# Issuing V from ACT's queue beside K on SP's queue in a streaming attention kernel

## The chip, the cores and the metric

The kernel runs on one core of a Trainium2 chip. The metric is the device time of one launch in microseconds (us). Ratios are computed as the mean time of one kernel's runs over the mean of the other's runs of the same rounds, so they are not quite the ratios of the medians that are quoted.

## The reference, cut to what matters

```python
# x: (2, 1, 512); k_cache, v_cache: (2, 32, 8192, 128), bf16
xn = layernorm(x)
q  = (xn @ wq).reshape(2, 1, 32, 128).transpose(0, 2, 1, 3)
p  = softmax(einsum("bhqd,bhkd->bhqk", q, k_cache) * 128 ** -0.5)
o  = einsum("bhqk,bhkd->bhqd", p, v_cache)
return x + merge_heads(o) @ wo + relu(xn @ w1) @ w2
```

It is a decode step: one query per batch and head, against 8192 keys and values. The two caches are 268 MB, the weights about 12 MB, and every byte is used once. So the question is how well the transfers are kept going.

## The kernel before

The 64 heads are done in 32 pairs. For each pair, K is 4 MB and V is 4 MB, each loaded by one transfer of 128 rows of 32 KB. There are two buffers for K (`ks`) and two for V (`vs`). TensorE works in steps: step t transposes K of pair t, computes the scores, and in its second half does the weighted sum with V of pair t-1. SP issues the transfers:

```python
load_k(0); load_k(1); load_v(0)
for t in range(NP - 2):                 # NP = 32
    sp.wait_ge(pT[NG - 1], t + 1)       # transposes of pair t are done: its K buffer is free
    load_k(t + R)                       # R = 2
    sp.wait_ge(sW, t + 1)               # weighted sum in step t is done: a V buffer is free
    load_v(t + 1)
sp.wait_ge(sW, NP - 1)
...                                     # V of pair 31 in two halves, then wo in five pieces
```

TensorE's step and its tail, cut:

```python
pe.wait_ge(dK[r], n16)                  # K of this pair has landed
for e in range(NG):
    transposes(r, e)
    if e >= 2: scores(r, e - 2, n)
values(v, n, n16)                       # waits for the softmax and for V of the pair before
weighted(v, 0) ...                      # and the last two groups of scores
# after the loop: two small sums, weighted(V of pair 31), transposes, product with wo
```

ACT's loop, in which the softmax of a pair and the copy of the result before it are done:

```python
with a.Fori(0, NP // R) as tr:
    for r in range(R):
        a.reg_add(reg, reg, 1)
        pair(r, reg, tr * R + r)        # ends with out_copy, which waits for sW
```

## Time and profile before

| | before |
|---|---|
| time, median of all runs of the first comparison | 661.0 us (660.82 to 661.77, 6 runs) |
| span of the profiled run | 658.7 us |
| bytes read | 280.5 MB, on one DMA queue |
| period of a step, from step 6 on | 19.43 us |
| TensorE's wait for K | 67.8 us in 27 waits |

The prediction shows the lines. The DMA engines are busy from start to end, and TensorE waits a little for K in nearly each step. When reading such a page, look at what remains after the last large transfer has landed: only there does TensorE's work show in the time.

### The profile page before, as it was taken

The page shows a single profiled execution, that of the slowest core. Times are in us where ns is not written, and L with a number is a line of the kernel's source. Part 1 is how long each engine was busy: PE and PEld are TensorE (multiplying, and loading weights), DVE is VectorE, ACT ScalarE, POOL GpSimd, SP SyncE. Part 2 cuts the span into 40 slices and gives each one's busy share as a digit, 9 for nine tenths or more (in the row PEclk, how much of TensorE's full clock was granted, in tenths as well). Part 3 has the DMA queues.
Part 4 walks back from the last instruction along what each step waited for, and adds up shares of the span by engine and source line. Part 5 has one row for each costly group of instructions (what it writes and reads, how often), then busy time and mean ns, then how long its engine had stood idle before and what let it go on. Part 6 is the DMA issues. An engine that isn't in the chain of part 4 may idle for free.

```text
span 658.7 us, 26859 instructions
## 1 busy us (share of the span) xinstructions
PE 559.9 (85%) x12737; PEld 536.7 (81%) x12737; DVE 253.2 (38%) x436; ACT 255.8 (39%) x403; POOL 8.8 (1%) x46
## 2 busy tenths in 40 slices
PE   2897799998889978789878878987888898878897
PEld 0497798987889978789878878987888898878896
DVE  1144344443434434334433434443334443434341
ACT  1034344443433534244353434434343434433340
POOL 1000000000000000000000000000000000000000
PEclk9889999998998989899988989898899988989996
DMA  8999999999999999999999999999999999999996
GB/s 365 433 440 420 439 428 431 436 426 438 422 442 422 440 432 428 438 424 442 420 442 424 436 436 426 438 422 442 424 438 430 430 438 424 440 422 442 424 425 282
DMA packets 10542, 280.66 MB, mean 426 GB/s; under 512 B 1186, under 2 KB 1188, under 8 KB 1700
## 3 DMA queue, kind: packets, MB, share of 16 engines
q1 hardware_dynamic: 10528, 280.50, 99.1%
q8 instruction: 9, 0.15, 0.1%
q14 instruction: 1, 0.01, 0.0%
q10 hardware_dynamic: 4, 0.00, 0.0%
HBM read 280.50 MB, written 0.00 MB: 426 GB/s over the span
## 4 chain that ended last, share of the span: by engine, by line
DMA 58%; PE 37%; ACT 2%; issue 1%; SPq 1%; ACTq 0%; DVE 0%
DMA ks<-in_A_k_cache_dram 54%; PE tp L288 21%; PE Sc L295 11%; PE ot L308 4%; DMA w_sb<-in_A_wo_dram 4%; ACT kT L415 2%; ACT L415 1%; SPq L190 0%; PE Sc L343 0%; SPq L185 0%; PE Sc L346 0%; SPq L173 0%; SPq L172 0%; SPq L166 0%; PE ot L400 0%
## 5 line engine op out<-in xcount | busy, mean ns | idle before, releaser
L288 PE MATMUL tp<-identb,ks 128*128 128x128 bf16 x4096 | 323.4, 228 | 67.8 <-DMA ks<-in_A_k_cache_dram 67.8
L415 DVE COPY kT<-tp 128x1024 bf16<-128x1024 bf16 x320 | 219.7, 691 | 323.8 <-PE tp L288 323.5
L288 PEld LDWEIGHTS tp<-identb,ks 128*128 128x128 bf16 x4096 | 255.0, 102 | 71.6 <-DMA ks<-in_A_k_cache_dram 71.5
L415 ACT COPY kT<-tp 128x1024 bf16<-128x1024 bf16 x192 | 194.3, 1012 | 231.2 <-PE tp L288 231.2
L295 PE MATMUL Sc<-q,kT 128*128 128x64 bf16 x4096 | 217.1, 196 | 9.3 <-ACT kT L415 6.1
L295 PEld LDWEIGHTS Sc<-q,kT 128*128 128x128 bf16 x4096 | 178.8, 100 | 13.1 <-ACT kT L415 9.6
L308 PE MATMUL ot<-prm,vs 128*128 128x64 bf16 x4224 | 157.6, 193 | 3.3 <-issue 3.3
L308 PEld LDWEIGHTS ot<-prm,vs 128*128 128x128 bf16 x4224 | 140.5, 98 | 6.2 <-issue 3.6
L528 ACT COPY nm<-Sc 128x2 f32<-128x2 f32 x32 | 5.1, 160 | 119.8 <-PE Sc L346 119.8
L532 ACT ACTIVATE prm<-Sc,nm 64x128 bf16<-64x128 f32 x64 | 25.7, 401 | 4.4
L469 DVE TENSOR_REDUCE mcol<-Sc 64x1 bf16<-64x128 f32 x64 | 18.6, 291 | 20.0 <-PE Sc L295 19.5
L415 ACT ACT_TABLE_LOAD x16 | 20.5, 1283 | 2.2
L243 PE MATMUL ot<-vs,xz 128*16 128x512 bf16 x32 | 8.6, 436 | 8.1 <-DMA vs<-in_A_wq_dram 8.1
L474 DVE TENSOR_REDUCE mx<-Sc 1x2 bf16<-1x128 bf16 x32 | 8.9, 279 | 16.9 <-PE Sc L343 16.9
L520 ACT COPY OTf<-ot 128x2 f32 x32 | 5.1, 160 | 26.1 <-PE ot L308 26.1
L243 PEld LDWEIGHTS ot<-vs,xz 128*16 128x16 bf16 x32 | 3.1, 99 | 13.1 <-issue 10.4
L228 POOL COPY q<-qb 128x2 bf16<-128x2 bf16 x32 | 5.8, 184 | 590.1 <-PE Sc L295 568.2
L532 ACT ACTIVATION_READ_ACCUMULATOR prm<-Sc,nm x64 | 11.8, 185 | 0.0
L445 DVE TENSOR_SCALAR qs<-ot 16x512 bf16<-16x512 f32 x1 | 0.7, 678 | 16.5 <-PE ot L243 16.5
L343 PE MATMUL Sc<-identb,mcol 128*1 128x128 bf16 x32 | 7.0, 217 | 0.0
L346 PE MATMUL Sc<-mx,onesb 1*128 1x2 bf16 x32 | 5.5, 172 | 0.0
L400 PE MATMUL ot<-OX,w_sb 128*128 128x2 bf16 x128 | 4.0, 166 | 1.1 <-DMA w_sb<-in_A_wo_dram 0.7
(56 smaller groups left out, 38.0 us busy)
## 6 DMA issues: line engine op xcount, KB each, us to landing
ks<-in_A_k_cache_dram SPq DMA_DIRECT2D x32, 4096.0 KB, 26.7
vs<-in_A_v_cache_dram SPq DMA_DIRECT2D x31, 4096.0 KB, 31.3
vs<-in_A_wq_dram SPq DMA_DIRECT2D x1, 4096.0 KB, 12.1
vs<-in_A_v_cache_dram SPq DMA_DIRECT2D x2, 2048.0 KB, 19.0
w_sb<-in_B_w_dram SPq DMA_DIRECT2D x2, 1792.0 KB, 17.9
w_sb<-in_A_wo_dram SPq DMA_DIRECT2D x1, 1792.0 KB, 25.1
w_sb<-in_A_wo_dram SPq DMA_DIRECT2D x1, 896.0 KB, 26.8
w_sb<-in_A_wo_dram SPq DMA_DIRECT2D x1, 768.0 KB, 28.2
```

The source lines that it names most:

```text
L228: g.tensor_copy(q2[t % R][:], qb[:, 2 * t:2 * t + 2]).then_inc(sQ1, 1)
L243: i = pe.matmul(qp, lhsT=xz[:, kt, Z - g * Bsz:Z - g * Bsz + QG * Bsz], rhs=vs[1][:, (kt * QG + g) * 512:(kt * QG + g + 1) * 512], start=( ...
L288: t = pe.transpose(tp[e % 4][:, i, :], ks[r][:, kk * Dh:(kk + 1) * Dh], identb[:])
L295: t = pe.matmul(Sc[r][:, 2 * kk:2 * kk + 2 * REP], lhsT=kT[e % 4][:, i, :], rhs=rep(q2[r][:]), start=True, stop=True,)
L308: t = pe.matmul(ot[r][:, 0:2 * REP], lhsT=vs[r][:, kk * Dh:(kk + 1) * Dh], rhs=rep(prm[r][:, kk, :]), start=(kk == 0), stop=(kk == KB - 1),)
L343: pe.transpose(tr_of(r), mcol[r][:], identb[:]).then_inc(sT, 1)
L346: pe.matmul(bc_of(r), lhsT=onesb[:], rhs=mx[r][:], start=True, stop=True).then_inc(sB, 1)
L415: fn(kT[e % 4][:], tp[e % 4][:]).then_inc(kR[e], 1)
L469: m = v.tensor_reduce(out=mcol[i][half, :], in_=S_of(i)[half, :, u], axis=AX.X, op=ALU.max)
L474: v.tensor_reduce(out=mx[i][:], in_=tr_of(i).rearrange("o (u m) -> o u m", u=2), axis=AX.X, op=ALU.max, negate=True,).then_inc(sX, 1)
L520: a.copy(OTf[:, bass.ds(c, 2)], ot[r][:, 0:2]).then_inc(sO, 1)
L532: x = a.activation(out=prm[i][half, :, u], in_=S_of(i)[half, :, u], func=ACTF.Exp, bias=nm[i][half, u:u + 1], scale=1.0, accum_out=RS[half ...
```

## The change

The intent is to put the two streams on two queues, so that V is issued by ACT, which has just waited for the same event, and SP has K alone. The whole diff, with some lines of its context cut:

```diff
@@ -177,8 +177,6 @@
         for t in range(NP - 2):
             sp.wait_ge(pT[NG - 1], t + 1)
             load_k(t + R)
-            sp.wait_ge(sW, t + 1)
-            load_v(t + 1)
         sp.wait_ge(sW, NP - 1)
@@ -543,10 +541,16 @@
-        with a.Fori(0, NP // R) as tr:
+        with a.Fori(0, NP // R - 1) as tr:
             for r in range(R):
                 a.reg_add(reg, reg, 1)
                 pair(r, reg, tr * R + r)
+                a.dma_start(
+                    vs[1 - r][:], V_all[bass.ds((tr * R + r + 1) * P, P), :]
+                ).then_inc(dV[1 - r], 16)
+        for r in range(R):
+            a.reg_add(reg, reg, 1)
+            pair(r, reg, NP - R + r)
```

## The prediction

> **What bounds the kernel now.** I read the page's slices and queues first, then the chain that ended last, then the timelines of the issuing queue and of TensorE. The slices and queues (tenths of busy time, GB/s, then packets, MB and share of 16 engines' span for each queue):
>
> ```profile
> DMA  8999999999999999999999999999999999999996
> GB/s 365 433 440 420 439 428 431 436 426 438 422 442 422 440 432 428 438 424 442 420 442 424 436 436 426 438 422 442 424 438 430 430 438 424 440 422 442 424 425 282
> q1 hardware_dynamic: 10528, 280.50, 99.1%
> q10 hardware_dynamic: 4, 0.00, 0.0%
> ```
>
> The DMA engines are full from the second slice to the last but one, at some 430 GB/s, and 99.1% of the engines' span went to one queue, SP's. ACT's queue (q10) carried only the small x load. The chain and the waits say who feels it:
>
> ```profile
> DMA 58%; PE 37%; ACT 2%; issue 1%; SPq 1%; ACTq 0%; DVE 0%
> PE tp L288 <- DMA ks<-in_A_k_cache_dram: 67.8, 27, 3.4
> ks<-in_A_k_cache_dram SPq DMA_DIRECT2D x32, 4096.0 KB, 26.7
> vs<-in_A_v_cache_dram SPq DMA_DIRECT2D x31, 4096.0 KB, 31.3
> ```
>
> TensorE waits for K 27 times, 67.8 us in all. It never waits for V. One step in the middle (start, duration, what; in brackets the idle time before it and its releaser):
>
> ```profile
> 314.64 1.34 PEld L288 LDWEIGHTS tp<-identb,ks 128*128 128x128 bf16 x24 [2.29 <-DMA ks<-in_A_k_cache_dram]
> ...
> 325.59 0.33 SPq L161 DMA_DIRECT2D ks<-in_A_k_cache_dram  x1
> ...
> 330.70 0.33 SPq L164 DMA_DIRECT2D vs<-in_A_v_cache_dram  x1
> 330.80 0.16 ACT L520 COPY OTf<-ot 128x2 f32 x1 [0.70 <-PE ot L308]
> 331.10 1.28 ACT L415 ACT_TABLE_LOAD   x1
> 334.07 2.48 PEld L288 LDWEIGHTS tp<-identb,ks 128*128 128x128 bf16 x24 [3.52 <-DMA ks<-in_A_k_cache_dram]
> ```
>
> A step starts at 314.64 when K has landed; the next starts at 334.07, 19.43 us later. Between them K and V move 2 x 4.194 MB, so the rate is 8.389 MB / 19.43 us = 431.8 GB/s and one 4 MB transfer takes 9.71 us. TensorE itself needs 16.06 us of the step (314.64 to 330.70). K is issued 10.95 us into the step, V at its end. All the steps from 139.81 us on have this period, within a few hundredths. The kernel is a stream of bytes; TensorE has about 2 to 3.5 us of slack per step. The tail matters too (TensorE's weight loads):
>
> ```profile
> 625.47 1.34 PEld L288 LDWEIGHTS tp<-identb,ks 128*128 128x128 bf16 x24 [2.32 <-DMA ks<-in_A_k_cache_dram]
> ...
> 641.85 0.52 PEld L363 LDWEIGHTS Sc<-RS,onesh 128*128 128x128 f32 x4 [0.48 <-issue]
> 642.41 0.96 PEld L366 LDWEIGHTS ot<-ident,ys 2*128 2x128 f32 x8
> 643.39 5.42 PEld L308 LDWEIGHTS ot<-prm,vs 128*128 128x128 bf16 x128
> ...
> 650.46 2.27 PEld L400 LDWEIGHTS ot<-OX,w_sb 128*128 128x128 bf16 x84 [0.44 <-DVE OX L501]
> 653.34 0.71 PEld L400 LDWEIGHTS ot<-OX,w_sb 128*128 128x128 bf16 x24 [0.62 <-DMA w_sb<-in_A_wo_dram]
> 654.26 0.40 PEld L400 LDWEIGHTS ot<-OX,w_sb 128*128 128x128 bf16 x12 [0.21 <-DMA w_sb<-in_A_wo_dram]
> 654.90 0.29 PEld L400 LDWEIGHTS ot<-OX,w_sb 128*128 128x128 bf16 x8 [0.24 <-DMA w_sb<-in_A_wo_dram]
> ```
>
> When the last K lands (625.47), three 4 MB transfers are still to come: V of pair 30, V of pair 31 and wo. 625.47 + 3 x 9.71 = 654.6, and the last wo piece lets TensorE go at 654.90. So TensorE's last work hides under the stream except for the last 3.8 us (span 658.7).
>
> **What the Trainium skill says.** (1) "DMA: Bandwidth & Descriptors", section "Issuing engines are not separate DMA queues": transfers started by SP, ACT or GpSimd run on the same 16 engines and interleave; issuing from several saves only the sequencer's issue time. The trace agrees in what it can show: an issue takes 0.33 us of SP's otherwise waiting queue, so there is nothing to save. (2) The same page, "Where 436 GB/s comes from": a ceiling of 435.2 GB/s for this fabric. The trace's 431.8 is within 0.8% of it. (3) The same page, "Queues, rings and completion order": each engine goes round-robin between the queues that have work, a packet at a time; and a completion increment lands only after all earlier writes of that engine, over its queues. The trace of before cannot show the first, having one busy queue only. I take it as equal halves, since the rows of K and V are equally long (32 KB).
>
> **The change, part by part.**
>
> Removed: 30 waits and 30 issues of V from SP. SP issues V after the wait for the same event (end of the weighted sum), which TensorE produces in order with the event for K. So SP's order never holds a K up behind a V wait: K was issued at 325.59, as the transposes ended, and V at 330.70, as the weighted sum ended. Worth 0.
>
> Added on ACT: per pair one issue. ACT's one DMA in this trace took 0.56 us, plus registers for the address; I estimate 0.5 to 0.8 us. It stands after the OTf copy (330.80 + 0.16), and ACT's next needed act is the first kT copy, some 0.7 us after TensorE restarts at 334.07. From 331.0: issue to 331.7, table load 1.28 us to 333.0. It is ready before 334.8. Worth 0 in the K-bound steps; V is issued about 0.5 us later than before, harmless with 31.3 us to landing. In the first steps, where TensorE is not yet waiting for K, the table load at 73.68 stood on the path, so one or two steps may lose about 0.5 us. Those steps regain it at the first K wait.
>
> Moved: the order of the bytes, and this is what counts. One queue is strict: K(t+2) goes before V(t+1). Check: from the start of step 0 at 32.82, the transfers up to K6 are eleven: 32.8 + 11 x 9.71 = 139.6; the first long run of K waits starts at 139.81. With two queues, K and V share, so V is served earlier and K later, while the total is the same.
>
> Worked from the issue times of before (K at 64.43, 85.26, 101.10; V at 52.33, 73.27, 90.36, 106.22): V0 is done at 52.2. K2 and V1 then share and end at about 71.6. V2 comes at 73.9, so K3 has 2.3 us alone and its other 7.4 us at half rate, 14.8 us: 88.7, still before the step needs it at 90.4. V2 has 2.3 us left and ends at 93.3; K4, which had 2.3, needs 14.8 more: 108.1. Step 3 ends at 106.2, so step 4 is the first to wait for K, where before it was step 6. From there both queues always have work, and each K takes 19.43 us. Last K: 108.3 + 27 x 19.43 = 632.9, against 625.47: 7.4 us later. V then lands at about K's landing + 4.6 us and is needed about 11 us after it, so V still makes nobody wait.
>
> Tail: the bytes end when they ended, at about 654.6. But TensorE's work after the last K, which was hidden, no longer is. From before: 625.47 to 641.37 the last step, 15.9; to 643.39, 2.0; V of pair 31, 5.42 and 0.38; to 650.46, 1.27; wo, 2.27 + 0.71 + 0.40 + 0.29 = 3.67; the end, 3.47. Sum 32.1. 632.9 + 32.1 = 665.0 against 658.7: +6.3 us. V31 would land at about 645 and wo at 654.6, before TensorE reaches them (about 651 and 658), so this sum has no DMA wait in it. By the sum: 660.88 + 6.3 = 667.2. I shade it to 666.0, because the share of K may exceed a half, and because a rate nearer to the 435 ceiling has a small chance.
>
> **Rivals.** (a) Nothing moves: the arbiter lets K's queue drain first, or the bytes alone decide. For: 99.1% of one queue, same bytes. Against: the tail argument needs only that V gets some earlier service. Time 660 to 661. (b) V is served first whenever it has work: then the whole of V30 stands before the last K, 9.71 us: 625.5 + 9.7 + 32.1 = 667.3 span, +8.6, 669.5 us. This bounds the ordering effect. (c) Two streams lower the rate (packet switches, two regions of HBM at once). One per cent of the roughly 525 us of K-bound steps is 5 us, on top: about 671; 2% would be 677. Nothing in this trace speaks for it, and nothing can against it, as no two large transfers on different queues meet here. (d) Two rings overlap better and reach 435.2: the steps shrink 0.8%, 4 us, giving about 663. (e) ACT's issue holds the kT copies up in each step: at most 0.8 us in 32 steps would be 26 us, but the 2.3 to 3.5 us idle before each K swallows it.
>
> **Range and chances.** Faster by 2% (under 647.7) would need more than the ceiling allows: 280.5 MB / 435.2 GB/s is 644.5 us before start and end are added. Chance 0.01. Slower by 2% (over 674.1) needs (c) at about 1.2% or more on top of the tail; 0.08. The range goes from (a), 660.5, to (b) with some loss of rate, 672.
>
> **What would show it.** ACT's queue should hold about 126 MB (30 x 4.19). K's time from issue to landing should stay near 27 us in the steady steps, V's fall from 31.3 to about 26, K waits start at step 4 (near 108 us), the period stay 19.43 us, and the last K land near 633. In the tail no wait for wo should be left: the chain ends in TensorE's L308 and L400. It is wrong if the period changes by over 0.1 us (rate), if the last K lands at 625 (no sharing), or if TensorE waits for V or for ACT's kT copies in the steady steps.

## The result, and the profile after

The changed kernel took 665.18 us (665.14 to 666.03, 6 runs), against 661.0 us before: ratio 1.0065, 95% interval 1.0052 to 1.0078. It is 4.2 us slower. The prediction said 666.0, in a range of 660.5 to 672.0.

The slices and queues of the changed kernel (as before: tenths busy, GB/s, then packets, MB and share of the engines' span), and its two large groups of issues (KB each, median us from issue to landing):

```profile
DMA  8999999999999999999999999999999999999994
GB/s 361 438 431 435 424 435 434 425 435 433 427 435 435 423 439 427 431 439 427 431 439 427 431 437 429 431 435 429 433 435 427 433 437 423 437 433 427 435 420 170
q1 hardware_dynamic: 6208, 154.67, 54.4%
q10 hardware_dynamic: 4324, 125.83, 44.1%
ks<-in_A_k_cache_dram SPq DMA_DIRECT2D x32, 4096.0 KB, 26.7
vs<-in_A_v_cache_dram ACTq DMA_DIRECT2D x30, 4096.0 KB, 28.6
```

ACT's queue now carries 125.83 MB (30 x 4.19). The rate in the slices is what it was, until the last slice: 170 GB/s where before it was 282, because the span now ends later than the bytes. K still takes 26.7 us to land; V takes 28.6 us instead of 31.3.

The first wait for K in the changed kernel, one step in the middle with ACT's issue, and the start of the last step (start, duration, what; in brackets the idle time and its releaser):

```profile
107.25 1.34 PEld L286 LDWEIGHTS tp<-identb,ks 128*128 128x128 bf16 x24 [0.49 <-DMA ks<-in_A_k_cache_dram]
...
319.04 0.34 ACTq L548 DMA_DIRECT2D vs<-in_A_v_cache_dram  x1
320.94 1.50 PEld L286 LDWEIGHTS tp<-identb,ks 128*128 128x128 bf16 x24 [2.31 <-DMA ks<-in_A_k_cache_dram]
...
340.36 1.34 PEld L286 LDWEIGHTS tp<-identb,ks 128*128 128x128 bf16 x24 [2.27 <-DMA ks<-in_A_k_cache_dram]
...
631.79 1.72 PEld L286 LDWEIGHTS tp<-identb,ks 128*128 128x128 bf16 x24 [2.41 <-DMA ks<-in_A_k_cache_dram]
649.28 0.52 PEld L361 LDWEIGHTS Sc<-RS,onesh 128*128 128x128 f32 x4 [0.39 <-issue]
...
650.82 3.96 PEld L306 LDWEIGHTS ot<-prm,vs 128*128 128x128 bf16 x128
...
656.42 3.27 PEld L398 LDWEIGHTS ot<-OX,w_sb 128*128 128x128 bf16 x128 [0.44 <-DVE OX L499]
```

The period is 340.36 - 320.94 = 19.42 us, as before; over all 27 steps from 107.25 to 631.79 it is 19.43. So no rate was lost. But the last K lands at 631.79 instead of 625.47, 6.3 us later, and from there TensorE's tail (31.3 us to the end at 663.1) is no longer hidden: the product with wo runs as one group of 128 without a wait for a piece of wo. The stretches of the end (us, then busy time of PE, PEld, DVE, ACT and POOL, the share of TensorE's full clock that it was granted, share of the DMA engines, GB/s), for the kernel before:

```profile
650.00:655.00 5.00, 3.86 (x127) 3.49 (x125) 0.23 (x1) 0.00 (x0) 0.00 (x0) 0.62 0.70 277
655.00:658.60 3.60, 0.55 (x9) 0.28 (x9) 0.38 (x2) 0.00 (x0) 0.00 (x0) 0.50 0.01 3
```

and for the changed kernel:

```profile
650.00:655.00 5.00, 4.90 (x136) 4.76 (x136) 0.79 (x3) 0.00 (x0) 0.00 (x0) 1.00 0.71 283
655.00:660.00 5.00, 3.93 (x134) 3.55 (x134) 0.77 (x4) 0.00 (x0) 0.00 (x0) 1.00 0.02 3
```

In both, the bytes end in the same stretch, with 277 and 283 GB/s. In the changed kernel TensorE is still at work, with 3.93 us of matmuls after 655, where before it had 0.55. The bytes are done as early as before; their order is worse.

### The profile page after: what moved, and what is told of

Read it like the earlier page. It is cut to its first block, busy times and chain, and to the rows that moved or that the text cites. A ratio compares the mean times of both kernels' runs of the same rounds, so it can differ in the third digit from the quotient of the medians.

```text
span 663.1 us, 26912 instructions
## 1 busy us (share of the span) xinstructions
PE 562.3 (85%) x12737; PEld 538.2 (81%) x12737; DVE 253.3 (38%) x436; ACT 254.5 (38%) x402; POOL 8.9 (1%) x46
## 3 DMA queue, kind: packets, MB, share of 16 engines
q10 hardware_dynamic: 4324, 125.83, 44.1%
## 4 chain that ended last, share of the span: by engine, by line
DMA 61%; PE 35%; ACT 2%; issue 1%; ACTq 0%; SPq 0%; DVE 0%
DMA ks<-in_A_k_cache_dram 61%; PE tp L286 20%; PE Sc L293 10%; PE ot L306 3%; ACT kT L413 1%; PE ot L398 1%; ACT L413 0%; ACTq L548 0%; PE ot L364 0%; PE Sc L361 0%; PE Sc L341 0%; SPq L173 0%; PE Sc L344 0%; SPq L172 0%; SPq L166 0%
## 5 line engine op out<-in xcount | busy, mean ns | idle before, releaser
L306 PEld LDWEIGHTS ot<-prm,vs 128*128 128x128 bf16 x4224 | 139.0, 97 | 7.9 <-issue 5.2
L518 ACT COPY OTf<-ot 128x2 f32 (+1 forms) x32 | 5.1, 160 | 27.8 <-PE ot L306 27.8
L530 ACT ACTIVATION_READ_ACCUMULATOR prm<-Sc,nm (+1 forms) x64 | 11.8, 185 | 0.0
L443 DVE TENSOR_SCALAR qs<-ot 16x512 bf16<-16x512 f32 x1 | 0.7, 679 | 18.1 <-PE ot L241 18.1
L271 PE MATMUL Sc<-w_sb,hT 128*2 128x512 bf16 x14 | 5.8, 600 | 0.1
## 6 DMA issues: line engine op xcount, KB each, us to landing
ks<-in_A_k_cache_dram SPq DMA_DIRECT2D x32, 4096.0 KB, 26.7
vs<-in_A_v_cache_dram ACTq DMA_DIRECT2D x30, 4096.0 KB, 28.6
w_sb<-in_B_w_dram SPq DMA_DIRECT2D x2, 1792.0 KB, 18.1
```

The lines of the kernel that those rows point to most:

```text
L271: i = pe.matmul(y, lhsT=hT[:, j, :], rhs=w2_sb[:, j, :], start=(j == 0), stop=(j == FJ - 1),)
L306: t = pe.matmul(ot[r][:, 0:2 * REP], lhsT=vs[r][:, kk * Dh:(kk + 1) * Dh], rhs=rep(prm[r][:, kk, :]), start=(kk == 0), stop=(kk == KB - 1),)
L530: x = a.activation(out=prm[i][half, :, u], in_=S_of(i)[half, :, u], func=ACTF.Exp, bias=nm[i][half, u:u + 1], scale=1.0, accum_out=RS[half ...
```

## The experiments

**Theory "order".** The transfers are a fixed amount at a fixed rate. What matters is how many bytes of V that are not needed yet go ahead of the last K. With two queues V30 takes part of the rate before the last K is done. **Rival "cost per transfer".** Two streams, or the issue on ACT, cost each pair a little, 4.2 us / 30 = 0.14 us. Each kernel below gave correct results. The kernel before took 660.86 to 660.98 us (medians) in their rounds. Where a landing of K is read from the start of the step that waited for it, the landing itself, read from the issue's own record, is within 0.1 us of it.

**One transfer undone: V30 back on SP's queue.** The other 29 stay on ACT's.

```diff
             load_k(t + R)
+            if t == NP - 3:
+                sp.wait_ge(sW, t + 1)
+                load_v(t + 1)
 # ACT: the loop is two pairs shorter; of the unrolled pairs only the first issues (V29)
```

> The change with one transfer undone: V of pair 30 goes back to SP's queue, behind the last K; V of pairs 1 to 29 stays on ACT's queue. Theory 'order' (only the bytes of V30 that go ahead of the last K cost time): the last K lands near 625.5 us, where it landed before, and the time is 661.0, within 0.7. Rival 'cost per transfer' (two streams or ACT's issues cost about 4.2/30 = 0.14 us each): 665.0. The period is 19.43 us in both.

Measured: 663.22 us (662.39 to 663.68, 5 runs), ratio 1.0033. Neither number. The last two steps of its trace:

```profile
614.40 2.47 PEld L289 LDWEIGHTS tp<-identb,ks 128*128 128x128 bf16 x24 [3.52 <-DMA ks<-in_A_k_cache_dram]
...
631.12 1.36 PEld L289 LDWEIGHTS tp<-identb,ks 128*128 128x128 bf16 x24
```

Step 30 starts 8.3 us later than before (606.05), and the last step then starts with no wait at all. K had landed at 626.50 (20.6 us after its issue at 605.93), but TensorE was not ready: it can make up only what its own work is shorter than a period. The expectation had forgotten that. This run alone decides nothing; the run with five transfers undone, below, is its repair.

**The opposite: V30 alone on ACT's queue.**

```diff
-            sp.wait_ge(sW, t + 1)
-            load_v(t + 1)
+            if t < NP - 3:
+                sp.wait_ge(sW, t + 1)
+                load_v(t + 1)
 # ACT: after pair 29, and only there:
+            if t + 1 == NP - 2:
+                a.dma_start(vs[1 - r][:], V_all[(t + 1) * P:(t + 2) * P, :]).then_inc(dV[1 - r], 16)
```

> The opposite: the kernel before with V of pair 30 alone issued from ACT's queue. Theory 'order': V30 finds ACT's queue empty, takes half of the rate from 604 us on and is done before the last K, so the last K lands 9.7 us later than before, near 635.2, and the time is 635.2 + 31.3 (the tail of the changed kernel) + 2.1 = 668.6, within 1.5: one transfer costs more than the thirty did. Pair 30's weighted sum may also wait some 8 us for V29. Rival 'cost per transfer': 661.1.

Measured: 668.76 us (667.41 to 669.5, 4 runs), ratio 1.0116. From its page (busy us, mean ns, then idle us before and what ended most of it) and its trace:

```profile
L309 PE MATMUL ot<-prm,vs 128*128 128x64 bf16 x4224 | 157.6, 193 | 11.6 <-DMA vs<-in_A_v_cache_dram 7.1
624.37 0.46 PEld L309 LDWEIGHTS ot<-prm,vs 128*128 128x128 bf16 x8 [7.24 <-issue]
635.23 1.96 PEld L289 LDWEIGHTS tp<-identb,ks 128*128 128x128 bf16 x24 [4.05 <-DMA ks<-in_A_k_cache_dram]
```

The last K lands at 635.23, where the theory put it (635.2). One transfer costs 7.9 us where thirty cost 4.2. That excludes a cost per transfer as the cause. The 7.24 us before the weighted sum of step 30 are the expected wait for V29: the weight loads name no releaser ("issue"), but for the matmuls the page names V (7.1 us).

**V first on one queue, from pair 4 on.** SP waits for the weighted sum, issues V(t+1), and only then K(t+2).

```diff
+            if t >= 4:
+                sp.wait_ge(sW, t + 1)
+                load_v(t + 1)
             sp.wait_ge(pT[NG - 1], t + 1)
             load_k(t + R)
-            sp.wait_ge(sW, t + 1)
-            load_v(t + 1)
+            if t < 4:
+                sp.wait_ge(sW, t + 1)
+                load_v(t + 1)
```

> No second queue at all: SP issues everything, but from pair 4 on V(t+1) before K(t+2). Theory 'order': the whole of V30 stands ahead of the last K, which lands near 635.2; time 668.6, within 1. Rivals that need the second queue or ACT's issue: 661.0.

Measured: 692.53 us (690.25 to 697.78, 6 runs), ratio 1.049. The expectation missed by 24 us, and the page shows where:

```profile
GB/s 368 442 431 424 427 433 434 435 428 380 433 441 388 439 390 426 372 426 448 401 426 405 414 410 426 426 376 426 376 420 445 435 369 422 428 363 435 416 372 121
```

Slices fall to 363 to 390 GB/s, again and again. Now K is issued at the end of a step with V, and the two together are 19.4 us of work: a step in which TensorE is late leaves the DMA engines without any. Where the pair was issued 4.5 us or more before the K before it landed, the next step took 19.4 to 19.8 us; where it was issued less than 3.4 us before, 19.4 to 22.5. This is another effect (too little issued ahead), and the total says nothing on the theory. The first step after the change of order does: step 6 starts at 149.70 instead of 139.81, 9.9 us or about one transfer later. Another 23 us gather in the 25 steps after it (20.35 us in the mean instead of 19.43), and they show what the two separate issue points of the kernel before are worth.

**ACT issues, but nothing moves.** V stays on SP's queue; ACT issues a tiny transfer at the same place.

```diff
+                a.dma_start(
+                    scr[:, bass.ds((tr * R + r) * 64, 64)],
+                    V_all[bass.ds((tr * R + r + 1) * P, 16), 0:64],
+                ).then_inc(dD, 16)
```

> The kernel before, and ACT issues in each of pairs 0 to 29, at the place where the change issues V, a transfer of the same form but of 16 rows of 128 bytes into a scratch tile. It measures ACT's issue and the second queue without moving V. Theory 'order': 661.0 to 662.5 (thirty tiny transfers may cost the DMA engines up to 1.5 us). Rival 'ACT's issue holds up kT copies': 665.

Measured: 661.93 us (661.74 to 662.17, 5 runs), ratio 1.0017. That is 1.1 us over the kernel before. The last step starts at 626.46 instead of 625.47, which fits about 1 us of the DMA engines' time for the tiny transfers in all. ACT's issues are not the 4.2 us.

**Queues exchanged: K from ACT, V from SP.**

```diff
 # SP: only the V part of the loop stays; ACT, after its last kT copy of a pair:
+            if k is not None:
+                a.wait_ge(pT[NG - 1], n)
+                a.dma_start(ks[i][:], K_all[k, :]).then_inc(dK[i], 16)
```

> Queues exchanged: K of pairs 2 to 31 from ACT's queue (issued at the end of the transposes, as before), V on SP's. Theory 'order' with equal shares: as the changed kernel, 665.2 within 1, last K near 632. If one of the two queues were favoured by the DMA engines, the last K would land earlier or later than in the changed kernel by the difference of shares; a rival in which ACT's queue is served faster gives 662 to 663 here.

Measured: 666.39 us (665.49 to 668.23, 5 runs), ratio 1.0089. That is 1.2 us above the expected 665.2, just outside its margin of 1. The last K lands at 633.13, a little later than the changed kernel's 631.79. Neither queue is favoured in the steady steps: from 127.9 to 633.1 us SP's queue holds 50.4% of the DMA engines' time and ACT's 49.9%. What differs is the start-up, told below in the section on the prediction.

**V issued later.** From pair 5 on, ACT issues V(t) in the middle of pair t.

```diff
+            if v is not None:                    # in pair(), after ACT's last kT copy
+                a.dma_start(vs[i][:], V_all[v, :]).then_inc(dV[i], 16)
```

> The changed kernel with V issued later: from pair 5 on ACT issues V(t) in the middle of pair t, after its last kT copy (some 11 us after K's landing and 13 us later than the change does). V is then barely in time. Theory 'order': V30 gets half of the rate for only 8.4 us before the last K lands, so 4.2 us of it goes ahead instead of 6.3: last K near 629.7, time 629.7 + 31.3 + 2.1 = 663.1, within 1, that is faster than the changed kernel by issuing later. If V comes too late, TensorE waits for V in each pair by up to 2 us, which the wait for K swallows. Rival 'cost per transfer': 665.2 or more.

Measured: 665.08 us (664.02 to 666.77, 6 runs), ratio 1.0063: a miss by 2 us, and the number that the rival gave (665.2). The trace decides between them. From the page, what TensorE's matmuls of the weighted sum waited for; from the trace, the last weighted sum that had to wait and the last step:

```profile
L306 PE MATMUL ot<-prm,vs 128*128 128x64 bf16 x4224 | 175.4, 202 | 68.6 <-DMA vs<-in_A_v_cache_dram 64.4
626.60 0.44 PEld L306 LDWEIGHTS ot<-prm,vs 128*128 128x128 bf16 x8 [3.48 <-issue]
...
632.90 1.36 PEld L286 LDWEIGHTS tp<-identb,ks 128*128 128x128 bf16 x24
```

The waits for K are gone from the steady steps, and in their place TensorE waits about 2.1 to 3.5 us for V in each before the weighted sum (V takes 22.9 us from issue to landing). So V became the transfer that sets the step. The order of the bytes did what the theory said: the last K landed at 628.92 (24.1 us after its issue at 604.86), near the expected 629.7. But V29 landed only at 626.5, so step 30 ended late and the last step began at 632.90, 4.0 us after its K. The wait was exchanged, not removed.

**Five transfers undone: V26 to V30 back on SP's queue.** The repair of the first experiment.

```diff
             load_k(t + R)
+            if t + 1 > 25:
+                sp.wait_ge(sW, t + 1)
+                load_v(t + 1)
 # ACT issues V1 to V25
```

> The first experiment (only V30 back on SP's queue) gave 663.2 instead of 661.0. In its trace the last step starts at 631.12 with no wait for K at all: step 30 had started 8.3 us later than in the kernel before, and TensorE can make up only the 2 to 3.5 us of a step by which its own work is shorter than the period. Here V26 to V30 are back on SP's queue and V1 to V25 stay on ACT's. Theory 'order' with that limit: the lag of 6 to 8 us is made up in the steps 27 to 29, the last K lands near 625.5 with a wait for it, and the time is 661.0, within 0.7. Rival 'cost per transfer' (25 of 30 remain): 664.5.

Measured: 661.44 us (660.87 to 663.57, 4 runs), ratio 1.0017, so the cost of the change is gone but for 0.5 us, with 25 of 30 transfers still on ACT's queue. The steps 26 to 29 of its trace:

```profile
535.63 1.34 PEld L289 LDWEIGHTS tp<-identb,ks 128*128 128x128 bf16 x24 [2.28 <-DMA ks<-in_A_k_cache_dram]
551.47 1.36 PEld L289 LDWEIGHTS tp<-identb,ks 128*128 128x128 bf16 x24
567.37 1.34 PEld L289 LDWEIGHTS tp<-identb,ks 128*128 128x128 bf16 x24
586.80 2.48 PEld L289 LDWEIGHTS tp<-identb,ks 128*128 128x128 bf16 x24 [3.53 <-DMA ks<-in_A_k_cache_dram]
```

In the kernel before these four started at 528.33, 547.76, 567.18 and 586.61. The lag is 7.3, 3.7, 0.2 and 0.2 us: two steps run without a wait at TensorE's own pace (15.84 and 15.90 us) and make it up. The last K lands at 625.65.

**One queue, V30 alone ahead of the last K.** The clean form of "V first".

```diff
+            if t == NP - 3:
+                sp.wait_ge(sW, t + 1)
+                load_v(t + 1)
             sp.wait_ge(pT[NG - 1], t + 1)
             load_k(t + R)
-            sp.wait_ge(sW, t + 1)
-            load_v(t + 1)
+            if t < NP - 3:
+                sp.wait_ge(sW, t + 1)
+                load_v(t + 1)
```

> The kernel before with one issue moved on the one queue: V30 before the last K, instead of after it (V first in all pairs, the earlier experiment, left the DMA engines idle and told nothing). No second queue, no issue from ACT, and enough in the queue to keep the engines full. Theory 'order': the last K lands 9.7 us later, near 635.2, time 635.2 + 31.4 + 2.1 = 668.7, within 1, and no wait for V29. Rivals that need the second queue: 661.0.

Measured: 669.83 us (668.83 to 670.05, 4 runs), ratio 1.0128. That is 1.1 us above the expected 668.7, just outside its margin of 1.

```profile
635.59 2.48 PEld L292 LDWEIGHTS tp<-identb,ks 128*128 128x128 bf16 x24 [12.06 <-DMA ks<-in_A_k_cache_dram]
```

TensorE waits 12.06 us for the last K, in one wait. There is no second queue here and no issue from ACT, and 8.9 us are lost by the place of one transfer.

**Half and a quarter of V30 ahead.** The same with `cut = SLOT // 2` and `SLOT // 4` columns ahead of the last K, the rest after it:

```diff
+        sp.dma_start(vs[0][:, 0:cut], V_all[(t + 1) * P:(t + 2) * P, 0:cut]).then_inc(dD, 16)
+        load_k(t + R)
+        sp.wait_ge(dD, 16)
+        sp.dma_start(vs[0][:, cut:], V_all[(t + 1) * P:(t + 2) * P, cut:]).then_inc(dV[0], 16)
```

> As the run with V30 ahead of the last K on SP's queue, but only the first half of V30's columns goes ahead (2 MB); the second half follows the last K once the first has landed. Theory 'order': last K at 625.5 + 4.9 = 630.4, time 630.4 + 31.4 + 2.1 = 663.9, within 1.

Measured: 665.15 us (664.51 to 665.43, 4 runs), ratio 1.0059; last K at 630.53.

> The same with a quarter ahead (1 MB). Theory 'order': last K at 627.9; TensorE's tail would end at 627.9 + 31.4 = 659.3, just above the 658.7 at which the stream of bytes ends the kernel anyway: 661.4, within 0.7. It shows that the first 1.3 us of lateness of the last K are free.

Measured: 662.74 us (662.02 to 662.97, 4 runs), ratio 1.0023; last K at 628.05.

Last K against time, in one table:

| V30 ahead of the last K on SP's queue | last K lands | time | expected time |
|---|---|---|---|
| none (the kernel before) | 625.47 | 660.96 | |
| a quarter | 628.05 | 662.74 | 661.4 |
| half | 630.53 | 665.15 | 663.9 |
| all | 635.59 | 669.83 | 668.7 |

The landings are within 0.4 us of the expected ones. The times lie 1.1 to 1.3 us above, all three just outside their margins. In these three profiles the tail from the last K to the end is 32.4 to 32.9 us instead of the 31.4 I had put in. In the half and quarter runs V31's group of 128 weight loads takes 5.42 us as it did in the kernel before, and in all three of these groups the granted clock is 0.68. In the whole-V30 run it takes 3.96 as in the changed kernel, both at a clock of 1.00; there the last step is the slow one, 18.1 us at a mean clock of 0.84, against 15.9 us at 1.00 in the kernel before. So where the slow spells of TensorE's clock fall moves the tail by about 1 us. What sets them off no run here shows. That the lateness of the last K is free up to 1.3 us is therefore not shown: the quarter, 2.6 us late, already cost 1.8.

None of these kernels beat the kernel before.

## Why the prediction was right

**What bounds the kernel.** Right. The period is 19.43 us in both kernels.

**The issues on ACT cost nothing in the steady steps.** Right: an issue took 0.34 us, and the run with tiny issues was only 1.1 us slower, as much as its last step starts later.

**The order of the bytes.** Right in kind: K waits begin at 107.25 (predicted 108), the last K lands at 631.79 (predicted 632.9). The size was off by 1.1 us: the lag (how much later the last steps start than in the kernel before) is 6.3 us, not 7.4. V's landing agrees with the measured lag, not with the predicted one. V was issued at 319.04 and took 28.6 us (the median), so it landed some 7.3 us after K's 340.36. At half rate those 7.3 us are 3.6 us of a transfer, so 9.7 - 3.6 = 6.1 us of V had gone ahead. The prediction had V land 4.6 us after K, and in about 26 us.

The term that was mis-sized is the start-up. The prediction let V1 share the rate at once, from 52.2. The trace has V1's issue at 51.77, but up to 55.2 only SP's queue moves bytes (1.51 MB, none on ACT's), so K2 had the engines alone until then. K2 landed at 69.58 and V1 at 76.38, where the prediction had both at 71.6; K4 landed at 107.20, where it had 108.1 (and 108.3 in the next sum, a slip of 0.2). In the steady steps the shares are equal, as predicted: from 126.7 to 631.7 us SP's queue holds 50.1% of the engines' time and ACT's 50.2%. A second error hid part of the first: the working used the issue times of before, and in the profile after, V2 was issued at 71.89 instead of 73.27. With the issue times of after and nothing else changed, the same working puts K4 at 109.9 (an estimate), a lag of some 9 us. So the nearness of 7.4 to 6.3 is in part luck.

The lag is not a fixed property of the change either: the first experiment, with the same code in the first steps, lagged by 8.3 us and the exchanged queues by 7.6 (both at step 30). In the first experiment's trace V2 was issued only at 76.14 and K4 at 88.39, and K's queue moved no bytes from 80.9 to 89.3 us, against 85.0 to 88.8 in the changed kernel. When TensorE finishes its first steps decides when each queue has work.

**The tail.** Right in kind: no wait for wo is left, and the tail after the last K is 31.3 us (predicted 32.1). Three terms were mis-sized, in opposite directions: the last step took 17.1 us instead of 15.9, V31 with what follows it 4.33 instead of 5.80, and wo 3.27 instead of 3.67.

**The rivals.** (a), nothing moves, and (d), a better rate, fell with the landing times and the period. (c), a loss of rate, and (e), a delay by ACT, fell with the period and the tiny issues. (b), V entirely ahead, was built on one queue: 669.83 against the 669.5 that the prediction gave it as the bound.

**The shading from 667.2 to 666.0** was made for a share of K above a half and a better rate. Neither came: the rate is the same and the steady shares are equal. The sum was 2.0 us too high for other reasons, 1.1 in the start-up and 0.8 in the tail, so that the shading went towards the measured number was luck.

What is shown by runs: the cost is that of V's bytes ahead of the last K (V30 alone does it with one queue or two, and the last K moves by 2.6, 5.1 and 10.1 us for a quarter, a half and all of it), and it goes away but for 0.5 us when V's last five transfers are put behind K again. A trial that undoes only the last one fails, because TensorE has to catch up too.

## What to carry to other kernels

Here the DMA engines were full, and a second queue brought no more bytes (19.43 us a step with one queue and with two); it only changed their order, from the order of issue to a mixture. Ask which transfer has the most work behind it at the end (here the last K, with 31 us of TensorE's work) and let nothing that is needed later share the rate with it. And check that a transfer which is moved behind another is still issued early enough to keep the queue full, and that the engine which lags has slack to catch up.

## What the Trainium skill lacked or had wrong

- "DMA: Bandwidth & Descriptors", sections "Issuing engines are not separate DMA queues" and "Rules for kernel authors": that spreading transfers over queues gives no bandwidth agrees with the runs (period 19.43 us in both, 431.8 GB/s under the stated ceiling of 435.2). What they lack: it is not neutral either. Two queues let later-needed bytes pass earlier-needed ones, here by 6.3 us at the last K and 4.2 us in the time; a single V transfer on the second queue cost 7.9 us.
- The same page, "Queues, rings and completion order": the round-robin between queues fits the steady steps, where each of the two queues holds 50% of the engines' time. That increments wait for earlier writes across queues, which the prediction also took from it, no run here shows. The page gives no word on how soon a queue gets its share when it starts while another keeps the engines full: V1's queue moved nothing for 3.4 us after its issue, and three kernels with the same streams ended their start-up with lags of 6.3, 7.6 and 8.3 us.
- No page that I used says how much must be issued ahead to keep a queue full when the consumer's time varies: two transfers issued together (19.4 us of work for a step of 19.43 us) let slices fall from about 430 to 363 to 390 GB/s, and cost some 23 us in 25 steps.
